# Weights and x in 128-row transfers in order of need, with block-1 transposes ahead of later loads

## The chip, the cores and the metric

The kernel runs on one core of one Trainium2 chip. The metric is device time in microseconds (us), the median over executions. The profiled span of an execution is shorter than its time (for instance 201.6 against 203.31).

## The reference, cut to what matters

```python
x = A_x                                   # (1, 2048, 512) bf16
xn = _layernorm(x, axis=-1)
return x + _A_ref(xn, A_wqkv, A_wo) + _B_ref(xn, B_w_in, B_w_sp, B_b_sp, B_w_out)
# _A_ref: qkv = xn @ wqkv, local dilated attention of 8 keys, @ wo
# _B_ref: z = gelu(xn @ w_in); z2 = layernorm(second half); spatial product; gate; @ w_out
```

Everything starts with the layernorm of x. A row of x must land, be normalized by VectorE and be transposed before the matrix engine (PE) can use it. The first products are q and k, then the second half of z ("z2").

## The kernel before: the parts that matter

x is held as four blocks; each block is four pieces of 128 rows, 128 KB each. SP and ACT issue the loads.

```python
for tb in range(2):                       # pieces 1 and 2 of block 0, in halves of 64 KB
    load_x0(SP, tb, 0)
    load_x0(A, tb, 1)
for tb in range(2, TB):                   # pieces 3 and 4, on the ACT queue
    A.dma_start(xall[:, 0, tb], xblk[0][:, tb])
load_wqk(SP, 0, 0, 2)                     # q weights, 256 KB
load_wqk(SP, 0, 2, 4)                     # q weights, 256 KB
SP.dma_start(xall[:, 1, 0:2], xblk[1][:, 0:2])    # half of x block 1, 256 KB
load_wqk(SP, 1)                           # k weights, 512 KB
SP.dma_start(xall[:, 1, 2:4], xblk[1][:, 2:4])
for j in range(2, 4):
    SP.dma_start(xall[:, j], xblk[j])     # x blocks 2 and 3, 512 KB each
SP.dma_start(w_z2[:], ...)                # z2 weights, 688 KB
```

The start of the computation, after pieces 1 and 2 of block 0. `ln_stats` and `ln_apply` run on VectorE, `ln_root` (the reciprocal root), `tr_copy` and `qk_copy` on ScalarE, `tr` and `qk_part` on PE; `tr_dma` is a transpose by DMA, issued by SP.

```python
for n in range(2, 4):
    ln_stats(t0[n]); ln_root(col(t0[n]))
for n in range(2, 4):
    ln_apply(t0[n])
...
qk_part(pqs[0], 0, 0, 0, 2, ...)          # q, pieces 1 and 2
tr_copy(t0[2], tr(t0[2]))                 # PE's second transposes
qk_part(pqs[1], 0, 1, 0, 2, (0,))
tr_copy(t0[3], tr(t0[3]))
qk_part(pqs[1], 0, 1, 0, 2, (1,))
qk_part(pqs[2], 0, 2, 0, 2)               # the first use of the k weights
for n in range(2):
    ln_stats(i1[n])                       # statistics of x block 1
ln_root(slice(1, 8, 4))
ln_stats(i1[2]); ln_apply(i1[0]); ln_apply(i1[1]); ln_stats(i1[3])
for n in range(2):
    qk_part(pqs[n], 0, n, 2, 4)
    qk_copy(pqs[n], 0, n)                 # evictions of q
ln_root(slice(9, 16, 4))                  # the last two roots, after both evictions
ln_stats(i2[0])
for n in range(2, 4):
    ln_apply(i1[n]); tr_dma(i1[n])
... # cut: rest of block 0, then block 1 (q and k), then z2 and everything else
```

Of the kernel before, what the change touches and what calls it, by code (L numbers as in the profile page):

```python
# [15 lines left out]
P = 128  # L16
S = 2048
D = 512
# [3 lines left out]
C = D // P  # L22
# [5 lines left out]
F = 1376  # L28
FH = 688
# [10 lines left out]
ORD = [1, 2, 3, 0]  # L40
# [31 lines left out]
def kernel(  # L72
# [17 lines left out]
    SP = nc.sync  # L90
# [3 lines left out]
    xblk = x2.rearrange("(b j p) d -> j p b d", b=TB, j=4)  # L94
# [9 lines left out]
    xall = r_x[:, 0:4 * TB * D].rearrange("p (j b d) -> p j b d", j=4, b=TB)  # L104
    vp = r_x[:].rearrange("p (d t) -> p d t", d=DH)
    r_w = sb.tile([P, 8192], BF16, name="r_w")
    wqk = r_w[:, 0:4096].rearrange("p (s k f) -> p s k f", s=2, k=C)
# [3 lines left out]
    QE = C * S  # L111
    r_qk = sb.tile([P, QE + C * (HALO + S)], BF16, name="r_qk")
# [26 lines left out]
    w_z2 = sb.tile([P, C, FH], BF16, name="w_z2")  # L139
# [27 lines left out]
    def load_x0(E, tb, h):  # L167
        E.dma_start(xall[:, 0, tb, 256 * h:256 * h + 256], x2[tb * TBS:tb * TBS + P, 256 * h:256 * h + 256])  # L168

    def load_wqk(E, s, k0=0, k1=C):  # L170
        E.dma_start(wqk[:, s, k0:k1],
                    A_wqkv[:, s * D:(s + 1) * D].rearrange("(k p) f -> p k f", p=P)[:, k0:k1])

    for tb in range(2):
        load_x0(SP, tb, 0)
        load_x0(A, tb, 1)
    for tb in range(2, TB):
        A.dma_start(xall[:, 0, tb], xblk[0][:, tb])
    load_wqk(SP, 0, 0, 2)
    load_wqk(SP, 0, 2, 4)  # L180
    SP.dma_start(xall[:, 1, 0:2], xblk[1][:, 0:2])
    load_wqk(SP, 1)
    SP.dma_start(xall[:, 1, 2:4], xblk[1][:, 2:4])
    for j in range(2, 4):
        SP.dma_start(xall[:, j], xblk[j])
    SP.dma_start(w_z2[:], B_w_in[:, FH:F].rearrange("(k p) f -> p k f", p=P))


    V.memset(warm[:, 0:P], 0.0)
# [17 lines left out]
    def ln_stats(i, parts=1):  # L207
        j, tb = i % 4, i // 4
        w = D // parts
        for h in range(parts):  # L210
            V.bn_stats(stats[:, i, 6 * h:6 * h + 6], xall[:, j, tb, w * h:w * h + w])  # L211
        V.bn_aggr(mv[:, i, :], stats[:, i, 0:6 * parts])

    def ln_root(sl):
        A.activation(rstd[:, sl], mv[:, sl, 1], ACT.Abs_reciprocal_sqrt, bias=eps_t[:])

    def ln_apply(i):
        j, tb = i % 4, i // 4
        V.tensor_scalar(xall[:, j, tb, :], xall[:, j, tb, :], mv[:, i, 0:1], rstd[:, i:i + 1],
                        ALU.subtract, ALU.mult)  # L220

    def tr(i):
        j, tb = i % 4, i // 4
        pt = ps_aux.tile([P, C, P], BF16, name="pt", tag="aux")
        for c in range(C):
            PE.transpose(pt[:, c, :], xall[:, j, tb, c * P:(c + 1) * P], ident[:])  # L226
        return pt

    def tr_copy(i, pt, c0=0, c1=C):
        A.copy(xnT[:, c0:c1, i * P:(i + 1) * P], pt[:, c0:c1, :])  # L230

    def tr_dma(i):
        j, tb = i % 4, i // 4
        SP.dma_start_transpose(xnT[:, :, i * P:(i + 1) * P], xall[:, j, tb, :])
# [70 lines left out]
    def qk_part(pq, j, m, b0, b1, ccs=(0, 1), p0=None, kcs=range(C)):  # L305
        sd, c0 = m // 2, 2 * (m % 2)
        p0 = b0 if p0 is None else p0
        xv = xnT[:].rearrange("p k (b j t) -> p k b j t", b=TB, j=4)
        for cc in ccs:
            for kc in kcs:  # L310
                PE.matmul(pq[:, cc, p0 * P:(p0 + b1 - b0) * P], wqk[:, sd, kc, c0 + cc:D:C],  # L311
                          xv[:, kc, b0:b1, j, :], start=(kc == 0), stop=(kc == C - 1))

    def qk_copy(pq, j, m, b0=0, b1=TB, p0=None):
        sd, c0 = m // 2, 2 * (m % 2)
        p0 = b0 if p0 is None else p0
        if sd == 0:
            dst = qs[:, j, c0:c0 + 2, b0 * P:b1 * P].rearrange("p c (b t) -> p c b t", b=b1 - b0)
        else:
            dst = ks[:, c0:c0 + 2, HALO:HALO + S].rearrange("p c (b j t) -> p c b j t", b=TB, j=4)[:, :, b0:b1, j, :]  # L320
        cast = A.copy(dst, pq[:, :, p0 * P:(p0 + b1 - b0) * P].rearrange("p c (b t) -> p c b t", b=b1 - b0))  # L321
        if sd == 1:
            for i in k_reads[j]:
                tc.declare_no_dep(cast.ins, i, reason="other token columns of the same rows")
            k_casts[j].append(cast.ins)

    def qk_tile():
        return ps_mm.tile([P, 2, TBS], F32, name="pq", tag="mm")
# [146 lines left out]

    def load_xr(o):
        if o == 0:
            for tb in (0, 2):
                SP.dma_start(r_qk[:, QE + 4096 + tb * D:QE + 4096 + (tb + 2) * D].rearrange("p (b d) -> p b d", b=2),
                             xblk[ORD[0]][:, tb:tb + 2])  # L480
            return
        for tb in range(TB):
            i = 4 * tb + ORD[o]
            SP.dma_start((xl_t if o == 3 else xr_t)[tb], x2[i * P:(i + 1) * P, :])
# [68 lines left out]
    def blk(j):  # L553
        return [4 * tb + j for tb in range(TB)]

    def col(i):
        return slice(i, i + 1)
# [9 lines left out]
    t0, i1 = blk(0), blk(1)  # L567
    i2, i3 = blk(2), blk(3)
# [17 lines left out]
    pqs = [qk_tile() for _ in range(3)]  # L586
# [6 lines left out]
    qk_part(pqs[2], 0, 2, 0, 2)  # L593
    for n in range(2):
        ln_stats(i1[n])
    ln_root(slice(1, 8, 4))
    ln_stats(i1[2])
    ln_apply(i1[0])
    ln_apply(i1[1])
    ln_stats(i1[3])  # L600
    for n in range(2):
        qk_part(pqs[n], 0, n, 2, 4)
        qk_copy(pqs[n], 0, n)
    ln_root(slice(9, 16, 4))
    ln_stats(i2[0])
    for n in range(2, 4):
        ln_apply(i1[n])
        tr_dma(i1[n])
    qk_part(pqs[2], 0, 2, 2, 4, (0,))
    tr_copy(i1[0], tr(i1[0]))  # L610
    qk_part(pqs[2], 0, 2, 2, 4, (1,))
# [2 lines left out]
    pq3 = qk_tile()  # L614
    qk_part(pq3, 0, 3, 0, 4)
    qk_copy(pq3, 0, 3)
    for n in range(1, 4):
        ln_stats(i2[n])
    ln_root(blk_cols(2))
# [6 lines left out]
    pqs = [qk_tile() for _ in range(3)]  # L626
# [31 lines left out]
    def halo_zero():  # L658
# [10 lines left out]
             "G": g_mm, "Gi": g_bias, "U": u_mul, "T": u_tr, "A": lambda k: ap[k](),  # L669
             "O": out_heads, "Or": out_rest, "Oh": out_half, "Fe": out_evac, "F": out_add, "s": out_store, "end": last_adds,  # L670
             "halo": halo_zero, "wo": load_wo, "late": load_late, "xr": load_xr, "w": load_wsp}
    for tok in ORDER.split():
        name = tok.rstrip("0123456789.")
# [31 lines left out]
```

## Time and profile before

| | kernel before |
|---|---|
| time, median of 3 at the time of the forecast | 202.78 us (202.71 to 203.77) |
| span of the profiled execution | 201.6 us |
| PE busy | 197.2 us (98%) |
| VectorE busy | 185.4 us (92%) |
| PE's second transposes start | 8.67 us |
| first z2 matmul | 22.66 us |

PE is the bound. The chain of waits (the work that ended last, followed back) shows where it is not PE that sets the pace. Columns: start in us, duration in us, what.

```profile
1.74 4.71 DMA r_x<-in_A_x_dram
6.48 0.70 DVE stats L211
7.21 0.18 DVE mv L212
7.40 0.70 DVE stats L211
8.13 0.18 DVE mv L212
8.31 0.31 DVE r_x L219
8.67 0.40 PE pt L226 x4
...
14.11 4.35 PE pq L311 x32
18.46 0.87 PE pa L311 x8
19.33 3.49 PE pq L311 x32
22.82 3.50 PE pz L240 x24
```

From 8.67 us on the chain holds only PE until 196.70 us. Before that it is a load of x, the third piece of block 0, that takes 4.71 us from issue to landing, and then VectorE. The first z2 matmul is a good milestone: after it, PE has no gap, and span minus its start is nearly a constant, 201.6 - 22.66 = 178.94 us here. PE's own timeline has the two starts:

```profile
13.95 4.51 PE L311 MATMUL pq<-xnT,r_w 128*128 128x512 bf16 x32
22.66 3.66 PE L240 MATMUL pz<-w_z,xnT 128*128 128x344 bf16 x24
```

(The chain dates work a little later than the timeline, 22.82 against 22.66, because a step there starts where the one ahead of it ends; starts below are the timeline's.)

### The profile page before, as it was taken

What the parts mean: (1) busy time and instruction counts of PE and PEld (TensorE: products, weight loads), DVE (VectorE), ACT (ScalarE), POOL (GpSimd) and SP (SyncE); (2) the same over time, 40 slices, a digit from 0 to 9 for tenths busy, and PEclk for the clock granted to TensorE, in tenths of its full rate; (3) what the DMA queues carried; (4) which work ended last, traced back from release to release, by engine and by line L of the source; (5) the groups of instructions that cost most, each with busy time, mean ns of one, the idle gap of its engine ahead of it and who ended that gap; (6) DMA issues with size and microseconds to landing.
All of it is one profiled execution on the core that took longest, in us unless ns stands there. A gap on an engine that the chain in (4) does not pass through costs nothing.

```text
span 201.6 us, 4043 instructions
## 1 busy us (share of the span) xinstructions
PE 197.2 (98%) x1667; PEld 124.9 (62%) x1667; DVE 185.4 (92%) x261; ACT 106.9 (53%) x174; POOL 4.1 (2%) x14
## 2 busy tenths in 40 slices
PE   7899999999999999999999999999999999999994
PEld 2689856656656666666656666644666446664562
DVE  5799699999999999999979999999999999999815
ACT  3575999989999886080383285134712152121400
POOL 3000000400000000000000000000000000000000
PEclk9999999999999999999999999999999999999999
DMA  4994447000794000659949808991243998059363
GB/s 129 340 298 77 90 94 249 0 0 0 134 209 79 0 3 0 125 176 222 205 101 263 166 3 202 195 204 25 75 106 78 234 182 119 0 144 194 77 207 133
DMA packets 66306, 25.91 MB, mean 129 GB/s; under 512 B 56240, under 2 KB 66032, under 8 KB 66032
## 3 DMA queue, kind: packets, MB, share of 16 engines
q1 hardware_dynamic: 65568, 25.19, 55.3%
q10 hardware_dynamic: 720, 0.47, 0.7%
q8 instruction: 13, 0.21, 0.5%
q14 instruction: 5, 0.04, 0.1%
HBM read 10.13 MB, written 2.10 MB: 61 GB/s over the span
## 4 chain that ended last, share of the span: by engine, by line
PE 93%; DMA 2%; DVE 2%; issue 0%; ACTq 0%
PE pg L454 37%; PE pz L240 19%; PE pq L311 13%; PE po L537 8%; PE pv L415 7%; PE po L507 6%; DMA r_x<-in_A_x_dram 2%; PE pl L365 1%; DVE r_pr L525 1%; PE po L516 1%; PE pb L507 1%; DVE stats L211 1%; PE pt L226 1%; ACTq L168 0%; PE pa L311 0%
## 5 line engine op out<-in xcount | busy, mean ns | idle before, releaser
L454 PE MATMUL pg<-z,r_qk 128*128 128x344 bf16 x448 | 66.6, 309 | 0.0
L454 PEld LDWEIGHTS <-r_qk 128*128 128x128 bf16 x448 | 43.8, 98 | 21.8
L240 PE MATMUL pz<-w_z,xnT 128*128 128x344 bf16 x256 | 40.0, 309 | 0.0
L460 ACT ACTIVATE gs<-pg,b_col 128x688 bf16<-128x688 f32 x16 | 13.2, 834 | 48.2 <-PE pg L454 48.2
L429 DVE TENSOR_TENSOR r_pr<-r_x,r_w 128x2048 bf16<-128x2048 bf16 x32 | 38.4, 1219 | 0.3
L433 DVE TENSOR_TENSOR r_pr<-r_pr 128x2048 bf16<-128x2048 bf16 x28 | 34.0, 1218 | 0.4
L240 PEld LDWEIGHTS <-xnT 128*128 128x128 bf16 x256 | 24.6, 98 | 14.4 <-issue 1.9
L311 PE MATMUL pq<-xnT,r_w 128*128 128x256 bf16 (+1 forms) x176 | 29.1, 317 | 0.1
L345 DVE TENSOR_TENSOR r_pr<-r_qk 128x2048 bf16<-128x2048 bf16 x24 | 28.2, 1218 | 0.3 <-ACT r_qk L321 0.3
L311 PEld LDWEIGHTS <-r_w 128*128 128x128 bf16 x184 | 20.2, 114 | 7.4 <-DMA r_w<-in_A_wqkv_dram 0.6
L321 ACT CAST r_qk<-pq 128x1024 bf16<-128x1024 f32 (+1 forms) x16 | 15.4, 990 | 1.9 <-PE pq L311 1.9
L537 PE MATMUL po<-r_w,r_uz 128*128 128x512 bf16 x70 | 16.0, 379 | 0.0
L302 ACT ACTIVATE r_uz<-pz 128x688 bf16<-128x688 f32 x16 | 11.7, 742 | 7.3 <-PE pz L240 7.2
L507 PE MATMUL po<-r_lg,r_pr 32*128 32x512 bf16 x224 | 14.5, 375 | 0.0
L520 ACT CAST r_qk<-po 128x512 bf16<-128x512 f32 x12 | 6.4, 589 | 14.7 <-PE po L537 14.6
L415 PE MATMUL pv<-xnT,r_w 128*32 128x512 bf16 x256 | 14.2, 379 | 0.0
L537 PEld LDWEIGHTS <-r_uz 128*128 128x128 bf16 x85 | 8.1, 98 | 9.3 <-issue 1.1
L354 DVE TENSOR_TENSOR r_pr<-r_pr 128x4096 bf16<-128x4096 bf16 x6 | 13.6, 2286 | 0.0
L211 DVE BATCH_NORM_STATS2 stats<-r_x 128x6 f32<-128x512 bf16 (+1 forms) x18 | 10.9, 615 | 2.0 <-DMA r_x<-in_A_x_dram 2.0
L264 ACT ACTIVATE junk<-z 128x688 bf16<-128x688 bf16 x16 | 12.4, 776 | 0.1
L415 PEld LDWEIGHTS <-r_w 128*32 128x32 bf16 x256 | 9.5, 139 | 4.4
L258 ACT ACTIVATE z<-pz 128x688 bf16<-128x688 f32 x16 | 11.8, 738 | 0.8 <-PE pz L240 0.7
(82 smaller groups left out, 175.5 us busy)
## 6 DMA issues: line engine op xcount, KB each, us to landing
r_lg<-in_A_wo_dram SPq DMA_DIRECT2D x8, 256.0 KB, 4.8
out_dram<-r_qk SPq DMA_DIRECT2D x12, 128.0 KB, 2.7
w_z<-in_B_w_in_dram SPq DMA_DIRECT2D x2, 688.0 KB, 5.4
r_w<-in_A_wqkv_dram SPq DMA_DIRECT2D x2, 512.0 KB, 5.2
r_x<-in_A_x_dram SPq DMA_DIRECT2D x2, 512.0 KB
r_qk<-in_A_x_dram SPq DMA_DIRECT2D x8, 128.0 KB, 2.4
r_w<-in_B_w_out_dram SPq DMA_DIRECT2D x1, 640.0 KB, 5.6
r_w<-in_A_wqkv_dram SPq DMA_DIRECT2D x2, 256.0 KB, 5.3
```

The lines of the kernel that those rows point to most:

```text
L240: PE.matmul(pz[:, hh, 0:FHALF], xnT[:, kc, i * P:(i + 1) * P], wz[:, kc, hh * FHALF:(hh + 1) * FHALF], start=(kc == 0), stop=(kc == C - 1))
L311: PE.matmul(pq[:, cc, p0 * P:(p0 + b1 - b0) * P], wqk[:, sd, kc, c0 + cc:D:C], xv[:, kc, b0:b1, j, :], start=(kc == 0), stop=(kc == C - 1))
L321: cast = A.copy(dst, pq[:, :, p0 * P:(p0 + b1 - b0) * P].rearrange("p c (b t) -> p c b t", b=b1 - b0))
L345: prod = V.tensor_tensor(pr[g % 3][:, c].rearrange("p w b t -> p b w t"), q3.unsqueeze(2).broadcast_to([P, TB, 4, P]), k4, ALU.mult)
L354: V.tensor_tensor(pr[g % 3][:, 0:2], pr[g % 3][:, 0:2], pr[g % 3][:, 2:4], ALU.add)
L415: PE.matmul(pv[32 * tb:32 * tb + 32, dd, :], wv[:, kc, 2 * d2 + dd, :], xnT[:, kc, tb * TBS:(tb + 1) * TBS], start=(kc == 0), stop=(kc == ...
L429: V.tensor_tensor(pw_t[n], vp[:, :, off:off + P], a_sb[:, slot_w(w), ts].unsqueeze(1).broadcast_to([P, DH, P]), ALU.mult)
L433: V.tensor_tensor(pw_t[n] if dst is None else dst, pw_t[n], pw_t[m], ALU.add)
L454: PE.matmul(pg[:, hh, 0:FHALF], wsp[n][:, k, :], z2[:, k, hh * FHALF:(hh + 1) * FHALF], start=(k == 0), stop=(k == NT - 1))
L460: A.activation(gs[:], tiles.pop(("g", n))[:, :, 0:FHALF], ACT.Identity, bias=b_col[:, i:i + 1])
L507: PE.matmul(pc, op[32 * tb:32 * tb + 32, d, o * P:(o + 1) * P], wo_r[32 * tb:32 * tb + 32, d, cs], start=(d == 8), stop=False, tile_positi ...
L537: PE.matmul(pc, uT[:, o % 2, m, tb * P:(tb + 1) * P], wout[:, m, cs], start=False, stop=(m == MCH - 3))
```

## The change

The intent: smaller transfers in the order in which they are needed, so that x and the weights at the front land sooner; statistics and roots of block 1 piece by piece; the transposes of block 1 issued ahead of loads that are needed later.

```diff
-    load_wqk(SP, 0, 0, 2)
-    load_wqk(SP, 0, 2, 4)
-    SP.dma_start(xall[:, 1, 0:2], xblk[1][:, 0:2])
-    load_wqk(SP, 1)
-    SP.dma_start(xall[:, 1, 2:4], xblk[1][:, 2:4])
-    for j in range(2, 4):
-        SP.dma_start(xall[:, j], xblk[j])
-    SP.dma_start(w_z2[:], ...)
+    for sd in range(2):
+        for kc in range(C):
+            load_wqk(SP, sd, kc)          # 128 KB each: q, then k
+    load_x(1, 0, 4)                       # 128 KB each
+    load_x(2, 0, 4)
+    load_x(3, 0, 2)
... # cut
     for n in range(2):
         ln_stats(i1[n])
-    ln_root(slice(1, 8, 4))
-    ln_stats(i1[2])
-    ln_apply(i1[0])
-    ln_apply(i1[1])
-    ln_stats(i1[3])
+        ln_root(col(i1[n]))
     for n in range(2):
-        qk_part(pqs[n], 0, n, 2, 4)
-        qk_copy(pqs[n], 0, n)
-    ln_root(slice(9, 16, 4))
-    ln_stats(i2[0])
+        ln_apply(i1[n])
+    qk_part(pqs[0], 0, 0, 2, 4)
+    qk_copy(pqs[0], 0, 0)
+    for n in range(2, 4):
+        ln_stats(i1[n])
+        ln_root(col(i1[n]))               # now ahead of the second eviction
+    qk_part(pqs[1], 0, 1, 2, 4)
+    qk_copy(pqs[1], 0, 1)
     for n in range(2, 4):
         ln_apply(i1[n])
         tr_dma(i1[n])
+    load_x(3, 2, 4)
+    for kc in range(C):
+        SP.dma_start(w_z2[:, kc], ...)    # 172 KB each
... # cut
+    ln_stats(i2[0])                       # moved here, behind qk_copy(pq3, 0, 3)
```

The k weights, 512 KB, moved ahead of the first half of x block 1. The order on PE is unchanged.

More of the change, by code (lines that the diff above doesn't have):

```diff
@@ L168, in load_x0, with load_wqk @@
         E.dma_start(xall[:, 0, tb, 256 * h:256 * h + 256], x2[tb * TBS:tb * TBS + P, 256 * h:256 * h + 256])
-    def load_wqk(E, s, k0=0, k1=C):
-        E.dma_start(wqk[:, s, k0:k1],
-                    A_wqkv[:, s * D:(s + 1) * D].rearrange("(k p) f -> p k f", p=P)[:, k0:k1])
+    def load_wqk(E, s, k):
+        E.dma_start(wqk[:, s, k], A_wqkv[k * P:(k + 1) * P, s * D:(s + 1) * D])
     for tb in range(2):
@@ L178, with load_x @@
         A.dma_start(xall[:, 0, tb], xblk[0][:, tb])
-    load_wqk(SP, 0, 0, 2)
-    load_wqk(SP, 0, 2, 4)
-    SP.dma_start(xall[:, 1, 0:2], xblk[1][:, 0:2])
-    load_wqk(SP, 1)
-    SP.dma_start(xall[:, 1, 2:4], xblk[1][:, 2:4])
-    for j in range(2, 4):
-        SP.dma_start(xall[:, j], xblk[j])
-    SP.dma_start(w_z2[:], B_w_in[:, FH:F].rearrange("(k p) f -> p k f", p=P))
+    for sd in range(2):
+        for kc in range(C):
+            load_wqk(SP, sd, kc)
+    def load_x(j, b0, b1):
+        for tb in range(b0, b1):
+            SP.dma_start(xall[:, j, tb], xblk[j][:, tb])
+    load_x(1, 0, 4)
+    load_x(2, 0, 4)
+    load_x(3, 0, 2)
     V.memset(warm[:, 0:P], 0.0)
@@ L477, in load_xr @@
         if o == 0:
-            for tb in (0, 2):
-                SP.dma_start(r_qk[:, QE + 4096 + tb * D:QE + 4096 + (tb + 2) * D].rearrange("p (b d) -> p b d", b=2),
-                             xblk[ORD[0]][:, tb:tb + 2])
+            for b0, b1 in ((0, 2), (2, 4)):
+                SP.dma_start(r_qk[:, QE + 4096 + b0 * D:QE + 4096 + b1 * D].rearrange("p (b d) -> p b d", d=D),
+                             xblk[ORD[0]][:, b0:b1])
             return
@@ L608 @@
         tr_dma(i1[n])
+    load_x(3, 2, 4)
+    for kc in range(C):
+        SP.dma_start(w_z2[:, kc], B_w_in[kc * P:(kc + 1) * P, FH:F])
     qk_part(pqs[2], 0, 2, 2, 4, (0,))
```

## The prediction

> **What bounds the kernel now.** The matrix engine. The page has PE busy 197.2 of 201.6 us (98%) at full clock. The chain of waits is PE work without a gap from 8.67 to 196.70 us, and the list of waits shows no PE matmul waiting after 9 us. VectorE is 92% busy but waits 4.4 us near the end, so it has slack. The change reaches only the first 25 us, where PE can gain only before 8.67 us. The chain's first long link is a DMA: the third 128-row piece of x block 0, issued by ACT at 1.74 us, landed at 6.45 us (4.71 us; the 64 KB pieces before it took 2.2 to 2.4). It shared the DMA engines with 512 KB of q weights and two x transfers; half-microsecond stretches show 250 to 360 GB/s from 4 us on. VectorE waited 0.78 us for it (5.70 to 6.48 us). Then come two statistics, two applies, and PE at 8.67 us, 0.43 us idle. Between 6.9 and 8.2 us eight matmuls took 1.35 us where 0.87 is their rate elsewhere: weight loads waited 0.28 and 0.35 us for q weights.
>
> **What the change does.** Same bytes. (1) Weights and x come in 128-row pieces. An issue costs SP 0.44 us (about 0.3 MB/us), and each transfer waits for the eighth before it (eight semaphores; before's ninth transfer waited 0.5 us). Fewer bytes stand beside the x pieces. The Trainium skill, "DMA: Bandwidth & Descriptors", Issuing engines are not separate DMA queues, says that transfers of all issuers interleave on the same engines; 4.71 against 2.3 us agrees. My estimates: x piece 3 lands at 4.5 to 5.2 us, q weights by 6.4, x block 1 at 8.4 to 10. (2) Block-1 roots go piece by piece: ScalarE gets two more (0.3 us each), the last ahead of the second q eviction (0.97 us). (3) Block-1 DMA transposes issue from about 13 us instead of 14.55; then half of x block 3 and the z2 weights, landing by about 20 us, needed at 22. PE's order is unchanged.
>
> **On the critical path.** Upper bound: VectorE's 0.78 us, as nothing before 5.70 us gets faster. PE's second transposes go from 8.67 to about 7.9 us; the q-weight waits vanish inside that time. Part is given back at 14 to 17 us: ScalarE evicts in a row there (11.95 to 16.9 us in before, some 0.5 us to spare for PSUM buffers). PE comes 0.77 us earlier, but ScalarE's new root waits for statistics of x pieces landing at about 9.5 us, ahead of an eviction. Estimate: PE waits 0 to 0.4 us for transposed block 1 or a PSUM buffer. Net gain 0.35 to 0.77 us; I take 0.5. After that PE is full, so the shift reaches the end nearly whole.
>
> **Predicted:** 202.25 us (before 202.78), range 201.6 to 202.95. Faster by over 2%: 0.02; within 2%: 0.965; slower: 0.015.
>
> **What would show it.** Third statistics at about 5.7 us without DMA wait; that x piece landing in near 3 us instead of 4.71; transposes of piece 3 at about 7.9 us; no q-weight wait; first z2 matmul at about 22.2 us instead of 22.66; small PE waits at 14 to 17 us on ScalarE; PE end at about 196.2 us instead of 196.7.
>
> **What would make it wrong.** x block 1, paced by issue and the eight-semaphore window, landing after 9 us: PE stalls near 12 to 15 us, and the gain vanishes or turns to loss. z2 weights landing after 22 us. x piece 3 no faster because the queues share differently: gain zero. A full 0.8 us if ScalarE keeps up.

## More of the kernel before

The DMA side, in stretches of 2 us. The last two columns are the mean busy share of the DMA engines and GB/s.

```profile
6.00:8.00 2.00, 1.92 (x14) 1.17 (x11) 1.48 (x3) 1.40 (x4) 0.00 (x0) 1.00 0.98 310
8.00:10.00 2.00, 1.57 (x20) 1.25 (x18) 1.86 (x7) 1.12 (x3) 0.00 (x0) 1.00 1.09 375
10.00:12.00 2.00, 2.00 (x21) 2.00 (x20) 1.93 (x6) 0.69 (x3) 0.00 (x0) 1.00 1.10 350
```

The busy share is 0.98 to 1.10, so the engines have next to no idle time.

## The result, and the profile after

| | before | after |
|---|---|---|
| time, median of 6 | 202.93 us (202.71 to 203.77) | 203.67 us (203.10 to 203.89) |
| span of the profiled execution | 201.6 us | 202.0 us |
| PE's second transposes | 8.67 us | 7.81 us |
| first z2 matmul | 22.66 us | 23.10 us |
| end of PE's part in the chain | 196.70 us | 197.14 us |

The ratio is 1.0027 (95% interval 1.0004 to 1.005): within 2%, and on the slow side. A ratio here is the mean time of one kernel's fast runs over that of the other's of the same rounds, so it is not quite the ratio of the medians quoted. Executions in which one die ran at a lower clock are left out of the means.

The chain of waits of the changed kernel (in it line 212 is the statistics, 216 the root, 220 the apply, 231 the copy of a transpose, 322 the eviction, 312 the q and k matmuls):

```profile
1.74 3.47 DMA r_x<-in_A_x_dram
...
6.07 3.59 DMA r_x<-in_A_x_dram
9.68 0.71 DVE stats L212
...
12.98 0.59 DVE stats L212
13.60 0.19 DVE mv L213
13.82 0.29 ACT rstd L216
14.11 0.90 ACT r_qk L322
15.01 0.98 ACT xnT L231 x2
16.03 2.86 PE pq L312 x24
18.90 0.87 PE pa L312 x8
19.77 3.49 PE pq L312 x32
23.26 3.50 PE pz L241 x24
```

Read it from the front. The x piece that took 4.71 us now takes 3.47, and PE's second transposes start 0.86 us earlier, as intended. But the chain now goes through a later x piece, the first of block 1: issued at 6.07 us, landed at 9.66. From there it goes through four statistics on VectorE (with the second root and an apply between them), the root of the last piece, the eviction that stands behind that root in ScalarE's order (14.11 us), and the two copies of transposes behind the eviction. Then PE may go on, at 16.03 us. PE's own timeline shows the gap, with its length and its releaser in brackets:

```profile
13.08 1.89 PE L312 MATMUL pq<-xnT,r_w 128*128 128x512 bf16 x8
16.03 2.86 PE L312 MATMUL pq<-xnT,r_w 128*128 128x256 bf16 x24 [1.07 <-ACT xnT L231]
...
23.10 3.66 PE L241 MATMUL pz<-w_z,xnT 128*128 128x344 bf16 x24
```

The sum closes. From the first of the eight wide q matmuls to the first z2 matmul, before took 22.66 - 13.95 = 8.71 us and after takes 23.10 - 13.08 = 10.02 us. So 0.86 us were gained at the front and 1.31 lost here, net 0.45 us of loss, which is the shift of the first z2 matmul and of PE's end (0.44 each). After that PE has no gap in either.

The DMA side after, in the same stretches:

```profile
6.00:8.00 2.00, 2.00 (x18) 1.38 (x16) 1.85 (x6) 1.58 (x5) 0.00 (x0) 1.00 0.96 277
8.00:10.00 2.00, 2.00 (x24) 1.99 (x22) 0.39 (x2) 1.17 (x2) 0.00 (x0) 1.00 0.92 285
10.00:12.00 2.00, 2.00 (x21) 2.00 (x20) 1.86 (x6) 0.87 (x3) 0.00 (x0) 1.00 0.85 269
```

The 128 KB pieces move 269 to 285 GB/s where the large transfers moved 310 to 375 in before's profile (278 in the first of these stretches in e9, below, with the same large transfers). SP needs 0.47 us from one issue to the next here (ten x loads in 4.70 us), and 128 KB in 0.47 us is 279 GB/s. So the pace of issue may be what limits the rate, and the busy share of 0.85 to 0.96 fits that; no run tests it. The Trainium skill, "DMA: Bandwidth & Descriptors", Bandwidth, advises large transfers ("Batch DMAs to ≥1 MiB for ≥75% of peak"; its figures are for another issuing path); this agrees in direction. Whether this lower rate is what made x block 1 late is a question for the experiments; VectorE's 0.39 us of work between 8 and 10 us shows that it was late.

### The profile page after: what moved, and what is told of

The parts are those of the page before. It is cut to its first block, busy times and chain, and to the rows that moved or that the text cites. A ratio compares the mean times of both kernels' runs of the same rounds, so it can differ in the third digit from the quotient of the medians.

```text
span 202.0 us, 4060 instructions
## 1 busy us (share of the span) xinstructions
PE 197.1 (98%) x1667; PEld 125.1 (62%) x1667; DVE 185.3 (92%) x261; ACT 107.3 (53%) x176; POOL 3.1 (2%) x14
## 4 chain that ended last, share of the span: by engine, by line
PE 90%; DMA 3%; DVE 3%; ACT 1%; issue 1%; ACTq 0%; SPq 0%
PE pg L455 37%; PE pz L241 19%; PE pq L312 10%; PE po L538 8%; PE pv L416 7%; PE po L508 6%; DMA r_x<-in_A_x_dram 3%; DVE stats L212 1%; PE pl L366 1%; DVE r_pr L526 1%; PE po L517 1%; PE pb L508 1%; ACT xnT L231 0%; ACT r_qk L322 0%; ACTq L168 0%
```

## The experiments

Theory A: the time at which a load lands is set by the bytes ahead of it. The k weights ahead of x block 1 made block 1 late, and the roots ahead of the second eviction passed the lateness on to PE. Rivals: the extra roots and the new order cost the time by themselves (B); the landing alone does it (C); the pace of issue did it; the place of the block-1 transposes did it.

The milestones of all profiles, read from each timeline. "Lag" is the start of the block-1 statistics minus that of PE's second transposes. "Wait" is PE's wait for the copied transposes ahead of block 1.

| run | second transposes | block-1 statistics | lag | wait | first z2 | time, median | ratio to before (95%) |
|---|---|---|---|---|---|---|---|
| after, first profile | 7.81 | 9.68 | 1.87 | 1.07 | 23.10 | 203.67 | 1.0027 (1.0004 to 1.005) |
| a2_after_again | 7.80 | 9.56 | 1.76 | 0.94 | 22.97 | 203.62 | one execution |
| a3_after_timed | 8.15 | 9.44 | 1.29 | 0.49 | 22.86 | 203.43 | 1.0011 (0.9994 to 1.0028) |
| e1_order_alone | 7.73 | 9.03 | 1.30 | 0, k late | 23.27 | 203.48 | 1.0014 (0.9987 to 1.0042) |
| e2_loads_alone | 7.87 | 9.32 | 1.45 | 0 | 21.85, then waits | 203.92 | 1.0034 (1.0008 to 1.006) |
| e3_x1_ahead_of_k | 7.71 | 8.04 | 0.33 | 0 | 22.26 | 203.49 | 1.0007 (0.9982 to 1.0032) |
| e4_k_one_transfer | 8.19 | 9.78 | 1.59 | 0.79 | 23.20 | 204.21 | 1.0049 (1.002 to 1.0079) |
| e5_loads_all_first | 7.50 | 9.61 | 2.11 | 0 | 22.53 | 203.28 | 1.0009 (0.9992 to 1.0027) |
| e6_after_loads_first | 7.96 | 9.34 | 1.38 | 0.57 | 22.76 | 203.58 | 1.0023 (1.0003 to 1.0043) |
| e7_roots_after_eviction | 8.02 | 8.81 | 0.79 | 0 | 22.00, then waits | 203.45 | 1.002 (1.0 to 1.004) |
| e8_k_needed_later | 7.76 | 8.53 | 0.77 | 0 | 22.00 | 202.93 | 1.0017 (0.9974 to 1.006) |
| e8_again | 7.80 | 8.58 | 0.78 | 0 | 21.94 | 202.92 | 0.9984 (0.9967 to 1.0001) |
| e9_big_transfers | 7.79 | 8.57 | 0.78 | 0 | 22.03 | 202.65 | 0.9982 (0.9962 to 1.0001) |

The differences in time are near the scatter, so most of what follows rests on the milestones.

### e1_order_alone

The kernel before with the new order of statistics and roots; its loads are unchanged.

```diff
-    ln_root(slice(1, 8, 4))               # and the rest of the old order
+        ln_root(col(i1[n]))               # and the rest of the new order
```

> The new order of block-1 statistics and roots with the old loads. Theory A (the k weights ahead of x block 1, at 0.43 us of issue each, make x block 1 land late, and the roots placed before the second q eviction pass that lateness on to PE): with x block 1 landing at 8.4 us as in before, the order alone costs next to nothing, first z2 matmul at 22.6 to 22.8 us, time within 0.2 us of before. Rival B (the extra roots and the new order cost the time by themselves, whatever the loads): first z2 matmul at 23.3 us or later, time 0.5 to 1 us over before.

Measured: first z2 matmul at 23.27 us, outside what theory A said and near rival B's number, but for neither's reason. The loads are before's, yet they landed differently from the first profile of before: the third x piece was there in time (third statistics at 5.60 us, no wait), PE's second transposes started at 7.73 us, and PE then waited 1.36 us for the k weights, until 10.59 us. PE's timeline:

```profile
10.59 3.25 PE L311 MATMUL pq<-xnT,r_w 128*128 128x256 bf16 x28 [1.36 <-DMA r_w<-in_A_wqkv_dram]
```

PE did not wait for block 1, though it was late here too, with the k weights behind it: VectorE waited 0.87 us for its first half and began its statistics at 9.03 us. So this run says little about the order and a lot about the loads of before: the wait that the forecast was built on is not always there. It led to the repeated profiles of before below.

### e2_loads_alone

The changed kernel with the old order of statistics and roots.

```diff
-        ln_root(col(i1[n]))               # and the rest of the new order
+    ln_root(slice(1, 8, 4))               # and the rest of the old order
```

> The new loads with the old order of block-1 statistics and roots. Theory A (lateness passes through the root that stands before the second q eviction): the first statistics of x block 1 still start at about 9.65 us, but the evictions no longer wait for the last roots; PE waits 0.3 to 0.6 us in all between 12 and 18 us instead of 1.3, first z2 matmul at about 22.3 us, time about 0.8 us under after and 0.3 under before. Rival C (the landing alone costs it, the order is harmless): PE wait of about 1.1 us or more stays, first z2 matmul at 23.0 us or later, time as after. Rival B expects it faster than before by the whole 0.8 us.

Measured: block 1 late (statistics at 9.32 us), and yet no wait ahead of block 1: PE reached z2 at 21.85 us, 1.25 us before the changed kernel. So the new order is needed for the loss, and rival C falls. (The run puts back the whole old order. That the root is the part of it that counts is read from the chain of after, where the eviction follows the root, 13.82 and then 14.11 us.) But the time got worse, not better, because two more waits stood behind. PE's timeline:

```profile
13.14 4.51 PE L312 MATMUL pq<-xnT,r_w 128*128 128x512 bf16 x32
...
21.85 0.46 PE L241 MATMUL pz<-w_z,xnT 128*128 128x344 bf16 x2
22.60 3.67 PE L241 MATMUL pz<-w_z,xnT 128*128 128x344 bf16 x22 [0.30 <-DMA w_z<-in_B_w_in_dram]
26.57 3.62 PE L312 MATMUL pq<-xnT,r_w 128*128 128x512 bf16 x16 [0.30 <-DMA xnT<-r_x]
```

The z2 weights and then the block-2 transposes were late. SP stood at the block-1 transposes until 14.38 us, issued the z2 weights only from 18.11 us on, and the block-2 transposes from 20.07 us on. My expectation missed this second wall.

### e3_x1_ahead_of_k

```diff
+    load_x(1, 0, 2)                       # between the q and the k weights
     for kc in range(C): load_wqk(SP, 1, kc)
-    load_x(1, 0, 4)
+    load_x(1, 2, 4)
```

> The changed kernel with the first two pieces of x block 1 issued ahead of the four k weight pieces, nothing else. Theory A: their statistics start at about 8.2 us instead of 9.68, the PE wait of 1.07 us for the copied block-1 transposes goes to under 0.2; instead PE waits 0.4 to 0.7 us at about 9.3 us for the last k weights, landing near 10 us; first z2 matmul at 22.3 to 22.6 us, time 0.5 to 0.8 us under after. Rival B: PE wait stays near 1 us, first z2 matmul at 23 us or later.

Measured: the block-1 statistics start at 8.04 us without waiting for a DMA, PE's wait ahead of block 1 is gone, and PE waits for the k weights instead (weight loads 0.5 us in all, the last until 9.91 us). First z2 matmul at 22.26 us. The new order of statistics and roots is in this run, so in this profile it costs PE no wait by itself: rival B falls. All as theory A had it, except the time: 203.49 us, within 0.2 us of after's (in another job). The spans of its six executions run from 201.3, the profiled one, to 202.2 us, so the profile caught a good draw.

```profile
8.04 0.69 DVE L214 BATCH_NORM_STATS2 stats<-r_x 128x6 f32<-128x512 bf16 x1
13.55 4.51 PE L314 MATMUL pq<-xnT,r_w 128*128 128x512 bf16 x32
```

### e4_k_one_transfer

```diff
-    for kc in range(C): load_wqk(SP, 1, kc)
+    SP.dma_start(wqk[:, 1], ...)          # 512 KB in one issue
```

> The changed kernel with the k weights in one transfer of 512 KB (one issue instead of four), x block 1 still behind them. If the pace of issue (0.43 us per 128 KB) made x block 1 late: its statistics start at 8.4 to 8.9 us instead of 9.68, the PE wait of 1.07 us falls to 0 to 0.4, first z2 matmul at about 22.2 us, time 0.8 us under after. If the bandwidth of the DMA engines made it late: statistics start at 9.4 us or later and the wait stays near 1 us.

Measured: the first piece of block 1 was issued at 4.18 us instead of 6.07, and landed at 9.76 instead of 9.66 us. It spent 5.58 us in the queue instead of 3.59. From the chain of waits, and the stretches of the DMA side:

```profile
4.18 5.58 DMA r_x<-in_A_x_dram
6.00:8.00 2.00, 1.32 (x12) 0.78 (x10) 1.93 (x6) 1.53 (x5) 0.00 (x0) 1.00 0.77 230
8.00:10.00 2.00, 2.00 (x24) 1.96 (x23) 0.27 (x2) 1.17 (x2) 0.00 (x0) 1.00 1.10 373
```

So an earlier issue alone did not bring it in earlier, with the same bytes ahead of it. But the run is no clean test of the pace: with the one large transfer the engines moved less from 6 to 8 us (230 against 277 GB/s), PE waited 0.31 us for q weights until 7.83 us, and the rate from 8 to 10 us was higher (373 against 285). Its time, 204.21 us, is the longest of all; the first z2 matmul, 0.1 us later than in after, does not explain that.

### e5_loads_all_first

e2 with the last half of x block 3 and the z2 weights issued with the other loads.

```diff
     load_x(3, 0, 2)
+    load_x(3, 2, 4)
+    for kc in range(C): SP.dma_start(w_z2[:, kc], ...)
... # and taken out behind the block-1 transposes
```

> The 128-row loads with the old order of statistics and roots (as in e2_loads_alone), and the last half of x block 3 and the z2 weights issued right behind the other loads instead of after the two block-1 transposes. Theory A2 (once the roots no longer hold the evictions, the next thing in the way is the sync engine, which reaches the z2 weights at 18 us and the block-2 transposes only at 20 us because it waits at the block-1 transposes): z2 weights and block-2 transposes come about 3 us earlier, PE has no wait over 0.2 us between 9 and 30 us, first z2 matmul at 21.8 to 22.1 us, second q stretch (block 2) at 25.3 to 25.6 us, time about 0.6 to 0.8 us under before. Rival: the z2 weights then slow the transposes or x on the shared DMA engines: PE waits stay, time not under before.

Measured: the second wall is gone (first z2 at 22.53 us, second q stretch at 26.03 instead of 26.57 us), but not all waits. PE waited 0.26 us for an apply of block 1, and until 19.01 us (0.27 us) for its DMA transposes, because block 1 landed at 9.59 us. The time is no better than before. The expectation was too high: late x block 1 has several ways to PE.

### e6_after_loads_first

The changed kernel with only the move of e5.

```diff
     load_x(3, 0, 2)
+    load_x(3, 2, 4)
+    for kc in range(C): SP.dma_start(w_z2[:, kc], ...)
... # and taken out behind the block-1 transposes; roots as in the changed kernel
```

> The changed kernel with only this moved: the last half of x block 3 and the z2 weights ahead of the block-1 transposes. Theory A2: the wait of about 1.1 us before block 1 at 15 us is made earlier, by x block 1 and the root before the eviction, and stays; first z2 matmul at 23.0 to 23.3 us, time as after (within 0.3 us). Rival (the place of the transposes is the cause of the loss): PE wait gone, first z2 matmul near 22 us.

Measured: wait 0.57 us, first z2 at 22.76 us, time 203.58 us. The wait neither vanished (the rival) nor stayed at 1.1 us. Its lag was 1.38 us, shorter than in the first profile of after. That gave the relation in the table: in every run with the changed kernel's block-1 order and its order of k ahead of x, wait = lag - 0.8 us (1.87 - 1.07, 1.76 - 0.94, 1.29 - 0.49, 1.59 - 0.79, 1.38 - 0.57). In all five, PE went on 6.34 to 6.35 us after those statistics began. So e6 is where the lag puts it, and this profile gives the place of the transposes no part in this loss.

### e7_roots_after_eviction

```diff
     for n in range(2, 4):
         ln_stats(i1[n])
-        ln_root(col(i1[n]))
     qk_part(pqs[1], 0, 1, 2, 4)
     qk_copy(pqs[1], 0, 1)
+    for n in range(2, 4):
+        ln_root(col(i1[n]))
```

> The changed kernel with only the roots of the third and fourth piece of block 1 moved behind the second q eviction. Theory A: statistics of x block 1 still start at about 9.6 us, but the PE wait before block 1 falls from 1.1 us to 0.2 to 0.5, first z2 matmul at 22.1 to 22.4 us; then the second wall of e2_loads_alone stands: a wait for block-2 transposes so that the second q stretch starts at about 26.4 us, and the time ends no better than before. If the landing alone counts: wait stays near 1 us.

Measured: no wait ahead of block 1, but block 1 landed early in this execution, with the same loads as in after: its first piece was issued at 6.32 us and landed at about 8.79, 2.5 us later.

```profile
8.81 0.70 DVE L212 BATCH_NORM_STATS2 stats<-r_x 128x6 f32<-128x512 bf16 x1 [0.45 <-DMA r_x<-in_A_x_dram]
```

With a lag of 0.79 us the unchanged order would not have waited either, so the run does not test the roots. e2 does: lag 1.45 us, where the changed order would wait 0.65, and no wait. The second wall stood here too (z2 weights until 23.06 us, 0.16 us).

### b2_before_again, b3_before_again, b4_before_again, a2_after_again

Both kernels unchanged, for more profiles.

> The kernel before, unchanged, for a second profile of it: how far the landing of the third piece of x block 0 (6.45 us in the first profile), of the k weights (9.95 us) and the first z2 matmul (22.66 us) move from run to run. I expect one of two forms: x early and PE waiting about 1 us for k weights at 9 to 10.5 us (as e1_order_alone showed with the same loads), or x late as in the first profile; first z2 matmul between 22.5 and 23.3 us.

> The kernel before, for a third profile. If the 0.78 us wait of the first profile was one draw of how transfers share the engines, PE's second transposes start between 7.7 and 8.7 us and the first z2 matmul at 22.2 to 23.3 us, mostly without the wait for the third x piece.

> The kernel before, a fourth profile, to see how often each form of its start occurs (third x piece late; k weights late with a PE wait of 1.2 us; neither). First z2 matmul anywhere between 22.2 and 23.3 us.

> The changed kernel again, for a second profile. Theory A expects the same picture: statistics of x block 1 start at 9.3 to 9.8 us, PE waits 0.5 to 1.3 us before block 1 at about 15 us, first z2 matmul at 22.7 to 23.3 us.

The kernel before starts in different ways:

| profile of before | third statistics | second transposes | PE's wait for k weights | first z2 | span |
|---|---|---|---|---|---|
| first | 6.48 | 8.67 | 0 | 22.66 | 201.6 |
| b2 | 6.21 | 8.27 | 0 | 22.25 | 201.2 |
| b3 | 5.63 | 7.81 | 1.18 | 23.16 | 202.1 |
| b4 | 5.57 | 7.80 | 0.24 | 22.21 | 201.2 |

In b2 the delay came from a 64 KB piece (3.23 us, landed at 4.50) and not from the third piece; neither form that I expected for b2 came, and its first z2 matmul lies below the 22.5 to 23.3 us that I gave. The chain of waits of b3, where the front was early:

```profile
3.31 7.13 DMA r_w<-in_A_wqkv_dram
10.44 0.05 issue
10.48 3.25 PE pq L311 x28
```

Here the k weights took 7.13 us and PE stood still until 10.48 us. So the chain of one profile named one load, and another load, the k weights, was almost as late behind it. In b3 and e1, where the first did not wait, the second cost more than the first ever did. The changed kernel looks steadier: its three profiles have the first z2 matmul at 23.10, 22.97 and 22.86 us. The means are 22.57 us for before and 22.98 us for after.

### e8_k_needed_later and e8_again

A version built on theory A: load order as in e3, all loads ahead of the block-1 transposes as in e5, roots as in e7, and PE does all q work of block 0 before its first use of the k weights.

```diff
-    tr_copy(t0[2], tr(t0[2]))
-    qk_part(pqs[1], 0, 1, 0, 2, (0,))
-    tr_copy(t0[3], tr(t0[3]))
-    qk_part(pqs[1], 0, 1, 0, 2, (1,))
-    qk_part(pqs[2], 0, 2, 0, 2)           # k weights
+    pt2, pt3 = tr(t0[2]), tr(t0[3])
+    V.tensor_copy(xnT[...], pt2[:])       # one copy on VectorE
+    tr_copy(t0[3], pt3)
+    qk_part(pqs[1], 0, 1, 0, 2)
... # q of pieces 3 and 4
+    qk_part(pqs[2], 0, 2, 0, 2)           # k weights, about 1.7 us later
     qk_part(pqs[2], 0, 2, 2, 4, (0,))
```

> A version meant to beat both, built on theory A (the time at which a load lands is set by the bytes issued ahead of it; 1.25 MB land by about 8 us, 1.75 MB by about 9.9 us). Loads in 128-row pieces: q, two pieces of x block 1, k, the rest of x, z2 weights, all issued before the block-1 transposes; PE does all q work of block 0 before it needs the k weights, which moves their need from 9.1 to about 10.8 us; VectorE copies one of the two late transposes; roots behind the second q eviction. Theory A: no PE wait over 0.2 us between 7 and 30 us, first z2 matmul at 21.8 to 22.1 us, time 0.4 to 0.7 us under before. If instead the landings follow something other than bytes ahead, k or x block 1 stalls PE again and z2 starts at 22.3 us or later.

> The version of e8_k_needed_later once more on one chip with the changed kernel, because two of its six executions and three of before's lay 1.5 us above the others. Theory A: first z2 matmul at 21.9 to 22.2 us again, span 200.9 to 201.2 us in most executions, time 0.5 to 0.9 us under the changed kernel and 0 to 0.5 us under before.

Measured: first z2 matmul at 22.00 and 21.94 us, with no PE wait over 0.2 us after 7 us. PE's timeline in e8_again:

```profile
7.80 0.74 PE L232 MATMUL pt<-ident,r_x 128*128 128x128 bf16 x8
8.38 4.09 PE L317 MATMUL pq<-xnT,r_w 128*128 128x256 bf16 x36
12.31 0.39 PE L232 MATMUL pt<-ident,r_x 128*128 128x128 bf16 x4
...
18.42 3.69 PE L317 MATMUL pq<-xnT,r_w 128*128 128x256 bf16 x32
21.94 3.66 PE L246 MATMUL pz<-w_z,xnT 128*128 128x344 bf16 x24
```

In the first, two of its six executions (and three of the eleven of before) lay about 1.5 us above the rest, so its interval is wide, and the 0.4 to 0.7 us under before that I expected did not show (medians 202.93 and 202.96). In the second its time was 202.92 us against 203.20 before.

### e9_big_transfers and a3_after_timed

e9 is e8's compute order with before's loads, sizes and order alike. a3 is the changed kernel, timed beside it.

```diff
-    for kc in range(C): load_wqk(SP, 0, kc)       # and the other 128-row loads
+    load_wqk(SP, 0, 0, 2)
+    load_wqk(SP, 0, 2, 4)
+    SP.dma_start(xall[:, 1, 0:2], xblk[1][:, 0:2])
+    load_wqk(SP, 1)                               # and the rest as in the kernel before
```

> The compute order of e8_k_needed_later with before's transfers (256 and 512 KB), to tell whether the 128-row pieces or the later need of the k weights brings the gain. Theory A (bytes ahead set the landing, the need decides the wait): k lands at 9.9 to 10.5 us against a need of about 10.7, no wait for it; first z2 matmul at 22.0 to 22.5 us, time within 0.3 us of e8_again; the third piece of x block 0 is late in some executions only. Rival (the pieces themselves matter): PE waits over 0.4 us for q weights, x or k, first z2 matmul at 22.7 us or later, time 0.5 us over e8_again.

> The changed kernel, timed beside the two others. Theory A: as before: PE wait of 0.8 to 1.3 us ahead of block 1, first z2 matmul at 22.8 to 23.3 us, time 0.3 to 0.8 us over the kernel before.

Measured: e9 has its first z2 matmul at 22.03 us, and no PE matmul waits over 0.2 us for q, k or x after 7 us; the k weights landed by 9.6 us at the latest (the last issue at 3.4 us plus the longest 6.2). PE's timeline in e9 from its second transposes on:

```profile
7.79 0.88 PE L226 MATMUL pt<-ident,r_x 128*128 128x128 bf16 x8
8.50 4.09 PE L311 MATMUL pq<-xnT,r_w 128*128 128x256 bf16 x36
...
22.03 3.66 PE L240 MATMUL pz<-w_z,xnT 128*128 128x344 bf16 x24
```

Times on one chip: e9 202.65, e8_again 202.92, before 203.20, a3_after_timed 203.43 us. e9's six runs (202.51 to 203.20) over a3's six (203.04 to 203.81) give 202.80 / 203.42 = 0.9969 by their means. Against before the interval of both e8_again and e9 just touches 1 (0.9982, 0.9962 to 1.0001, for e9). a3's wait ahead of block 1, 0.49 us, lies under the 0.8 to 1.3 us that I expected. So e9 and e8_again, which these runs do not tell apart (means 202.80 and 202.87), are the fastest versions run: 0.3% under after, and 0.2% under before, where the interval still holds 1. The 128-row pieces are not needed for it. The later need of the k weights is the part that meets the waits which the profiles of before show; the other parts of e9's order (the copy on VectorE, the roots) were not taken out one by one.

## Why the prediction was wrong

Forecast: 0.77 us gained at the front, 0 to 0.4 us given back, 0.5 us net, 202.25 us with an upper end of 202.95. Measured: 203.67 us.

1. **What bounds the kernel: right.** PE, with nothing to gain after the first z2 matmul. PE's end moved with that matmul, 0.44 us each.
2. **The front: right in the pair of profiles that was compared.** Third statistics at 5.56 us without a wait (forecast about 5.7), the x piece 3.47 us instead of 4.71 (forecast "near 3"), second transposes at 7.81 us (forecast 7.9).
3. **The front as a typical gain: too large.** "Upper bound: VectorE's 0.78 us" came from one profile. In b3, b4 and e1, with the same loads, the third piece was not late and the second transposes came at 7.73 to 7.81 us, as in the changed kernel; only then did the k weights make PE wait, 0.24 to 1.36 us. The forecast did not ask which load would be the next to be waited for.
4. **The step that failed: "Estimate: PE waits 0 to 0.4 us for transposed block 1 or a PSUM buffer."** In the profiled pair the mechanism was named rightly (ScalarE's root waits for late x statistics, ahead of an eviction); the size was off. The term was 1.31 us by the sum of starts (the profile's wait: 1.07, 0.94 and 0.49 us in three profiles). In a sum of 0.77 - 0.27 the second term, taken at 0.27, became 1.31; the first became 0.86.
5. **Why it was mis-sized.** The prediction gave "x block 1 at 8.4 to 10" and spoke of "x pieces landing at about 9.5 us". The relation wait = lag - 0.8 us says what these are worth, with the second transposes at the forecast 7.9 us: a first piece at 8.4 us gives no wait, one at 9.5 us gives 0.8 us, twice the upper end of the estimate. So 0 to 0.4 us fits only a first piece near the early end of the prediction's own range. I let it land at 8.4 us, about 2.3 us after its issue, as an undisturbed 64 KB piece does (the record does not spell this step out). It was issued at 6.07 us and landed at 9.66, 3.59 us later; the measured lags of 1.29 to 1.87 us gave waits of 0.49 to 1.07.
6. **What made it late: open in part.** The prediction's warning named pace and the eight-semaphore window. e4 took three issues away and the piece landed at 9.76 us, so an earlier issue alone was no cure (with the reservation above). Moving the piece ahead of the k weights (e3) had it there by 8.04 us. It fits that in after and in e4 this piece is the end of 1664 KB (x block 0, q, k and itself, 512 + 512 + 512 + 128), and in e3 of 1152 KB. But the bytes ahead do not fix the landing: with the same 1664 KB it came at 8.79 us in e7 and at 9.66 in after. A run that changes the bytes and nothing else was not made.
7. **z2 weights: right for after itself.** No wait for them there, because PE was late. Where PE came on time (e2, e7) they were late, as was warned.

In the profiled pair the loss is settled by the traces: the wait ahead of block 1. That this wait is what the medians lost is not shown: e2, e3 and e7 had no such wait in their profiles, and their medians (203.45 to 203.92 us) are no better than after's 203.67 and 203.43. In e2 and e7 other waits took its place; in e3 the wait for the k weights was smaller, and the profiled execution was the fastest of the six. The size in the pair is a draw too: against b3's first z2 matmul (23.16 us) that of after (23.10 us) would show no loss. The size of the loss in time stands against scatter of the same order, 1.0027 (1.0004 to 1.005) and 1.0011 (0.9994 to 1.0028). What decides which of its starts the kernel before takes in an execution stays open.

## What to carry to other kernels

When loads queue on busy DMA engines, moving one ahead can move another back: before promising the wait that the chain of waits shows, list the next loads with their landing and their need, because the second-latest load takes over (the k weights in b3 and e1, x block 1 in after). Take the landing of a queued transfer from several that the traces show in a queue, as a range, and not from one undisturbed transfer: the same piece took 2.5 us in e7, 3.6 in after and 5.6 in e4, where it was issued earlier. Profile the old kernel several times before a gain below 1 us is read from one execution. The fastest versions here let PE need the late weights later, and one of them kept the large loads. And on one engine, nothing that waits for a late load should stand ahead of an eviction that is ready, as the root did in after.

## What the Trainium skill lacked or had wrong

- "DMA: Bandwidth & Descriptors", Issuing engines are not separate DMA queues, says that starting DMAs from several engines saves only the sequencer's issue time, "which is usually small relative to the DMA itself". Beside the 3.3 to 3.8 us that a 128 KB piece took to land in after, 0.47 us from issue to issue is small, as it says. As a rate it need not be: 128 KB in 0.47 us is 279 GB/s, and the changed kernel moved 269 to 285 GB/s. That the pace of issue set this rate was not tested.
- The same page, Anatomy of one DMA, gives about 2.0 us fixed plus bytes over a rate for a transfer on another issuing path. The first 64 KB loads took 2.2 to 2.4 us in before and after, which agrees; one in b2 took 3.23 us. I found no figure on it for a transfer in a full queue: 3.3 to 3.8 us for the 128 KB pieces of after, 5.3 to 6.3 us for the weight transfers of 256 and 512 KB in before (up to 7.1 in b3).
- I found no page that says how far landings move between executions of one unchanged kernel: k weights in use from 9.53 to 10.59 us in b4, b3 and e1, and a first z2 matmul between 22.21 and 23.16 us in four profiles of before.
